# The last 24 units of a fused attention and feed-forward kernel in three chunks of 8, two of them with tokens on partitions

## The chip, the cores and the metric

The kernel runs on one core of a Trainium2 chip. The metric is device time in microseconds, the median of several runs. Beside it there is one profiled execution, with the times of every instruction and DMA piece; its own time is given with it.

## The reference

A polynomial-sketch attention feeds a feed-forward layer with a learned Swish. Cut to what matters here:

```python
batch, n_heads, seq, head_dim = (4, 4, 1088, 32)
attn_out = _attn_ref(q, k, v, S1, S2)                  # (4, 4, 1088, 32)
x = attn_out.transpose(0, 2, 1, 3).reshape(4352, 128)  # a token's four heads side by side

h = x @ w_in                                           # (4352, 128) @ (128, 2048)
g = h * (1.0 / (1.0 + np.exp(-beta * h)))              # beta: one for each of the 2048 columns
out = g @ w_out                                        # (4352, 2048) @ (2048, 128), f32
```

The attention phase makes `xall`, the 4352 tokens in f16 with the 128 model dimensions on partitions. The change lies in the second phase, the last three lines.

## The kernel before, in words

A sequence of 1088 tokens is cut into 34 units (`U`) of 32 tokens (`T`): token t of unit u is row `t * 34 + u` of the sequence. The four batches give 136 units. So 32 tokens of one unit lie 34 rows apart in the output, and rows of neighbouring units with the same t lie side by side.

The feed-forward phase works on chunks of units. `chunks` holds eight of 16 units (512 tokens) and a last one of 8 (256 tokens). A chunk has 16 blocks `j` of 128 hidden columns, handled in waves. A wave fills two PSUM banks, 1024 columns: two blocks of 512 tokens or four of 256. There are 68 waves in all: 64 of the first kind, 4 of the second.

- `first(s, w)`, steps `f<s>a` and `f<s>b`: half a wave each. TensorE multiplies `winb` (the input weights times beta) with `xall` into the PSUM tile `wave` (L705). After the b half ScalarE applies Silu to the 1024 columns and writes them as f16 into `gT` (L716). The very last wave is done in two Silus of 512 (L714). `wave` has two buffers.
- `second(s, w)`, steps `s<s>a` and `s<s>b`: half a wave of the product with `woutp`, summed over the 16 blocks in PSUM. For chunks of 16 units `woutp` is the stationary operand and the 512 tokens stream (L737); the result, in the tile `acc`, has model dimensions on partitions and tokens along the row. For the last chunk `gT` is stationary and the 128 columns of `woutp` stream (L729); the result, in the tile `fin` on two banks, has tokens on partitions, 128 in each bank.
- `store(ci)`, steps `o0` to `o8`. For a chunk of 16 units VectorE transposes `acc` in blocks of 32 by 32 into `osb` (L664). Then SP issues four DMAs, one for each 32 model dimensions (L670); a piece of them is 32 floats, 128 bytes. A chunk that crosses a batch boundary, such as chunk 6, takes two such groups, eight DMAs.
- `store_last`, step `o8`: ScalarE copies the first bank of `fin` and VectorE the second (L685), and each half goes out in one DMA (L686), the first on ScalarE's queue, the second on SP's. A piece is a whole row of 128 floats, 512 bytes. Partitions run over unit and then token, so the outer dimension of the output's access pattern is the 4 units and the next one the 32 tokens.

Nothing is left to a scheduler. `ORDER` is a list of step names written by hand, and each engine's program is the steps in that order. An engine stops at an instruction until the semaphores for its operands have come; instructions behind it on the same engine wait too. In the last part of `ORDER`, `f` steps run several waves ahead of the `s` steps, `o7` stands between `f67a` and `f67b`, and `s64a` to `s67b` and `o8` are last.

PSUM is full: `wave` takes two buffers of two banks, `att2` two banks, `acc` and `att1` one each. `fin` uses `att2`, which the attention phase has left by then.

Of the kernel before, what the change touches and what calls it, by code (L numbers as in the profile page):

```python
# [7 lines left out]
F32 = mybir.dt.float32  # L8
F16 = mybir.dt.float16
ALU = mybir.AluOpType  # L10
ACTF = mybir.ActivationFunctionType

P = 128
T = 32
# [3 lines left out]
def kernel(  # L18
# [12 lines left out]
    nc = tc.nc  # L31

    B, H, S, D = q.shape
    R = S1.shape[0]
    F = R * R
    NTOK, DM = out.shape
    DFF = moe_w_in.shape[1]
    NJ = DFF // P
    U = S // T
# [32 lines left out]
    f47a f47b s40b s41a s41b f48a f48b s42a s42b f49a f49b s43a s43b f50a f50b s44a s44b s45a f51a f51b s45b  # L72
    s46a f52a f52b s46b s47a s47b f53a f53b f54a o5 f54b s48a s48b s49a f55a f55b s49b s50a f56a f56b s50b s51a
    f57a f57b s51b s52a s52b f58a f58b s53a s53b f59a f59b s54a s54b s55a s55b f60a f60b f61a o6 f61b s56a s56b
    s57a s57b f62a f62b s58a s58b f63a f63b s59a s59b s60a f64a f64b s60b s61a f65a f65b s61b s62a s62b f66a
    f66b s63a s63b f67a o7 f67b s64a s64b s65a s65b s66a s66b s67a s67b o8
    """

    ENGINES = {
# [12 lines left out]
    ps = ctx.enter_context(tc.tile_pool(name="ps", bufs=1, space=bass.MemoryType.PSUM))  # L92
    ctx.enter_context(tc.manual_schedule())

    def ap(t, offset, dims, p0=0, pn=None):
        pd = list(t.ap[0])
        s = t if pn is None else t[p0 : p0 + pn]
        return bass.AP(tensor=s.tensor, offset=s.offset + offset, ap=[list(s.ap[0])] + dims)

    def ct(shape, dtype, name):  # L100
        return const.tile(shape, dtype, tag=name, name=name)
# [36 lines left out]
    att2_t = lambda n: ps.tile([P, 2, 512], F32, tag="att2", name=n)  # L138
    acc_t = lambda n: ps.tile([P, 512], F32, tag="acc", name=n)
# [501 lines left out]

    chunks = []
    u = 0
    for n in (16,) * 8 + (8,):
        chunks.append((u, n))
        u += n
    assert u == B * U and chunks[-1][1] == 8
    waves = []
    for ci, (u0, un) in enumerate(chunks):
        per = 1024 // (un * T)  # L650
# [2 lines left out]

    gts, accs, wvs = {}, {}, {}

    LAST = len(chunks) - 1

    def store(ci):
        u0, un = chunks[ci]
        if ci == LAST:  # L660
            store_last(u0, un)
            return
        osb = sb.tile([P, 16, T], F32, tag="osb", bufs=3, name="osb")
        nc.vector.transpose(out=osb[:, :un, :].rearrange("p u m -> p (u m)"), in_=accs[ci][:, : un * T])  # L664
        done = 0
        while done < un:
            b, u = divmod(u0 + done, U)
            n = min(un - done, U - u)
            for m in range(4):
                nc.sync.dma_start(  # L670
                    out=bass.AP(
                        tensor=out.tensor,
                        offset=out.offset + (b * S + u) * DM + m * T,
                        ap=[[U * DM, T], [DM, n], [1, T]],
                    ),
                    in_=osb[T * m : T * m + T, done : done + n, :],
                )
            done += n

    def store_last(u0, un):  # L680

        b, u = divmod(u0, U)
        for i, (copy, e) in enumerate(((nc.scalar.copy, nc.scalar), (nc.vector.tensor_copy, nc.sync))):
            o = ct([P, DM], F32, f"fin_sb{i}")
            copy(out=o, in_=accs[LAST][:, i, 0:DM])  # L685
            e.dma_start(  # L686
                out=bass.AP(
                    tensor=out.tensor,
                    offset=out.offset + (b * S + u + 4 * i) * DM,
                    ap=[[DM, 4], [U * DM, T], [1, DM]],  # L690
                ),
                in_=o,
            )

    def first(s, w):
        ci, n, per, j0 = waves[s]
        u0, un = chunks[ci]
        if s % GP == 0 and w == 0:
            gts[s // GP] = sb.tile([P, GP * 1024], F16, tag="gT", bufs=GB, name="gT")
        if w == 0:  # L700
            wvs[s] = wave_t("wave")
        half, g, o = per // 2, gts[s // GP], s % GP * 1024
        for i in range(half):
            j = j0 + w * half + i
            nc.tensor.matmul(  # L705
                out=wvs[s][:, w, i * n : i * n + n],
                lhsT=winb[:, j * P : j * P + P],
                rhs=xall[:, u0 * T : u0 * T + n],
                start=True,
                stop=True,  # L710
            )
        if s == len(waves) - 1 and w:
            for i in range(2):
                nc.scalar.activation(out=g[:, o + 512 * i : o + 512 * i + 512], in_=wvs[s][:, i], func=ACTF.Silu)  # L714
        elif w:
            nc.scalar.activation(  # L716
                out=g[:, o : o + 1024], in_=wvs[s].rearrange("p a n -> p (a n)"), func=ACTF.Silu
            )

    def second(s, w):  # L720
        ci, n, per, j0 = waves[s]
        if j0 == 0 and w == 0:
            accs[ci] = att2_t("fin") if ci == LAST else acc_t("acc")
        half = per // 2
        for i in range(half):
            j, o = j0 + w * half + i, s % GP * 1024 + w * 512 + i * n
            if ci == LAST:
                for a in range(2):
                    nc.tensor.matmul(  # L729
                        out=accs[ci][:, a, 0:DM],  # L730
                        lhsT=gts[s // GP][:, o + a * P : o + a * P + P],
                        rhs=woutp[:, j, :],
                        start=(j == 0),
                        stop=(j == NJ - 1),
                    )
                continue
            nc.tensor.matmul(  # L737
                out=accs[ci][:, :n],
                lhsT=woutp[:, j, :],
                rhs=gts[s // GP][:, o : o + n],  # L740
                start=(j == 0),
                stop=(j == NJ - 1),
            )

    for s in range(len(waves)):
        for w in range(2):
            step(f"f{s}{'ab'[w]}", first, s, w)
            step(f"s{s}{'ab'[w]}", second, s, w)
    for ci in range(len(chunks)):
        step(f"o{ci}", store, ci)  # L750
# [37 lines left out]
```

## Time and profile before

| | us |
|---|---|
| median of three runs | 104.2 (103.89, 104.2, 107.08) |
| profiled execution | 104.39 |
| its span, first to last instruction | 102.63 |
| TensorE busy in the span | 95.2 (93%) |
| ScalarE busy | 72.3 (70%) |
| VectorE busy | 59.1 (58%) |
| GpSimd busy | 40.7 (40%) |

The granted TensorE clock was 0.998 of full speed. The shares are means over two very different phases: GpSimd works in the attention phase alone, and in the last 20 us TensorE and ScalarE work with hardly a pause. The time outside the span, 1.75 us, is before the first and behind the last recorded instruction. A row of the groups reads: line, engine, operation, output and inputs, shapes, count, then busy time in us and mean ns of one, then the engine's idle time before these instructions and what ended it. A row of the DMA issues gives the KB of each and the median us from issue to landing. A matmul's duration in the rows is longer than its share of TensorE's time, since successive ones overlap; the distance between their starts is what counts.

### The profile page before, as it was taken

What the parts mean: (1) busy time and instruction counts of PE and PEld (TensorE: products, weight loads), DVE (VectorE), ACT (ScalarE), POOL (GpSimd) and SP (SyncE); (2) the same over time, 40 slices, a digit from 0 to 9 for tenths busy, and PEclk for the clock granted to TensorE, in tenths of its full rate; (3) what the DMA queues carried; (4) which work ended last, traced back from release to release, by engine and by line L of the source; (5) the groups of instructions that cost most, each with busy time, mean ns of one, the idle gap of its engine ahead of it and who ended that gap; (6) DMA issues with size and microseconds to landing.
All of it is one profiled execution on the core that took longest, in us unless ns stands there. A gap on an engine that the chain in (4) does not pass through costs nothing.

```text
span 102.6 us, 3065 instructions
## 1 busy us (share of the span) xinstructions
PE 95.2 (93%) x1294; PEld 45.0 (44%) x1294; DVE 59.1 (58%) x107; ACT 72.3 (70%) x92; POOL 40.7 (40%) x49
## 2 busy tenths in 40 slices
PE   5999989999999999999999999999999999999900
PEld 1234554344445454345446433644534444446800
DVE  1564888999798995898953967489240020200210
ACT  1412022687695984789995879999979999899710
POOL 6409689989997993008090000094000000000000
PEclk9999999999999999999999999999999999999999
DMA  2999999986661446613320261051004132022250
GB/s 50 321 255 306 394 378 386 246 270 134 248 217 32 90 127 174 169 27 64 94 70 13 43 114 60 0 101 39 6 13 70 19 52 50 0 44 49 44 101 25
DMA packets 24965, 12.56 MB, mean 122 GB/s; under 512 B 17992, under 2 KB 22648, under 8 KB 24952
## 3 DMA queue, kind: packets, MB, share of 16 engines
q1 hardware_dynamic: 24756, 12.29, 44.6%
q8 instruction: 10, 0.16, 0.7%
q10 hardware_dynamic: 196, 0.08, 0.3%
q14 instruction: 3, 0.02, 0.1%
HBM read 9.84 MB, written 2.23 MB: 118 GB/s over the span
## 4 chain that ended last, share of the span: by engine, by line
PE 86%; ACT 7%; DVE 1%; issue 1%; ACTq 0%
PE wave L705 27%; PE acc L737 24%; PE idle L340 9%; ACT gT L716 6%; PE at L520 6%; PE xp L571 5%; PE qpp L430 3%; PE kpp L357 2%; PE at L450 2%; PE fin L729 2%; PE at L393 2%; PE xw L571 1%; PE at L548 1%; PE at L407 1%; PE cb L393 0%
## 5 line engine op out<-in xcount | busy, mean ns | idle before, releaser
L716 ACT ACTIVATE gT<-wave 128x1024 f16<-128x1024 f32 x67 | 64.8, 1024 | 8.1 <-PE wave L705 7.5
L705 PE MATMUL wave<-xall,winb 128*128 128x512 f16 (+1 forms) x144 | 40.7, 368 | 0.4 <-DVE xall L588 0.2
L737 PE MATMUL acc<-gT,woutp 128*128 128x512 f16 x128 | 36.9, 379 | 0.0
L372 POOL TENSOR_TENSOR qp<-an,tq 128x768 f32<-128x768 f32 (+1 forms) x8 | 14.0, 1760 | 22.1 <-DVE an L496 22.1
L705 PEld LDWEIGHTS <-winb 128*128 128x128 f16 x144 | 13.4, 99 | 17.5 <-issue 3.9
L737 PEld LDWEIGHTS <-woutp 128*128 128x128 f16 x128 | 12.4, 98 | 14.9 <-issue 0.6
L664 DVE STREAM_TRANSPOSE osb<-acc 128x512 f32<-128x512 f32 x8 | 5.7, 714 | 21.1 <-PE acc L737 21.1
L372 POOL TENSOR_TENSOR kp<-tk 128x512 f32<-128x512 f32 (+1 forms) x12 | 15.0, 1276 | 6.4 <-DVE tk L368 6.4
L508 DVE STREAM_TRANSPOSE qpt<-qp 128x768 f32<-128x768 f32 (+1 forms) x13 | 11.1, 883 | 0.3 <-POOL qp L372 0.2
L340 PE MATMUL idle<-warm 128*128 128x512 f16 x30 | 9.6, 454 | 1.3 <-DVE tiny L231 1.3
L344 DVE STREAM_TRANSPOSE kT<-k_in 128x576 f32<-128x576 f32 (+1 forms) x8 | 5.6, 719 | 2.5 <-DMA k_in<-in_k_dram 2.5
L571 PE MATMUL xp<-qpt,kvr 32*32 32x288 f32 (+2 forms) x160 | 6.9, 364 | 0.0
L571 PE MATMUL xw<-qpt,kvr 32*32 32x256 f32 (+1 forms) x160 | 6.8, 343 | 0.0
L349 DVE STREAM_TRANSPOSE qT<-q_in 128x512 f32<-128x512 f32 (+1 forms) x8 | 5.8, 724 | 0.9 <-DMA q_in<-in_q_dram 0.9
L520 PE MATMUL at<-kp,v_in 128*32 128x64 f32 (+1 forms) x288 | 6.3, 223 | 0.0
L520 PEld LDWEIGHTS at<-kp,v_in 128*32 128x32 f32 (+1 forms) x288 | 4.7, 109 | 3.2 <-issue 1.7
L310 POOL TENSOR_TENSOR winb<-w_in_sb,beta_all 128x512 f16<-128x512 f32 x4 | 5.2, 1293 | 0.2 <-DMA beta_all<-in_moe_beta_dram 0.2
L340 PEld LDWEIGHTS <-warm 128*128 128x128 f16 x30 | 2.9, 110 | 4.5 <-issue 1.6
L571 PEld LDWEIGHTS xp<-qpt,kvr 32*32 32x32 f32 x160 | 3.7, 103 | 2.3 <-issue 0.8
L372 DVE TENSOR_TENSOR qp<-an,tq 128x768 f32<-128x768 f32 (+1 forms) x5 | 4.5, 906 | 0.1
L588 ACT CAST xall<-xw 128x128 f16<-128x128 f32 (+1 forms) x8 | 2.4, 325 | 3.0 <-PE xw L571 2.0
L473 DVE TENSOR_TENSOR prod<-tq,tcc 128x288 f32<-128x288 f32 (+2 forms) x5 | 4.1, 818 | 0.1
(75 smaller groups left out, 67.3 us busy)
## 6 DMA issues: line engine op xcount, KB each, us to landing
k_in<-in_k_dram SPq DMA_DIRECT2D x6, 272.0 KB, 5.3
q_in<-in_q_dram SPq DMA_DIRECT2D x6, 272.0 KB, 3.9
out_dram<-osb SPq DMA_DIRECT2D x20, 64.0 KB, 1.9
v_in<-in_v_dram SPq DMA_DIRECT2D x8, 144.0 KB, 4.0
v_in<-in_v_dram SPq DMA_DIRECT2D x8, 128.0 KB, 3.0
w_in_sb<-in_moe_w_in_dram SPq DMA_DIRECT2D x4, 256.0 KB, 4.8
beta_all<-in_moe_beta_dram SPq DMA_DIRECT2D x4, 256.0 KB, 6.9
w_out_sb<-in_moe_w_out_dram SPq DMA_DIRECT2D x4, 256.0 KB, 6.1
```

The source lines that it names most:

```text
L310: eng(name).tensor_tensor(out=winb[:, s], in0=w_in_sb[:, s], in1=beta_all[:, s], op=ALU.mult)
L340: nc.tensor.matmul(out=t[:, 0, :], lhsT=warm[:, 0:P], rhs=warm, start=True, stop=True)
L344: nc.vector.transpose(out=kT[:, u0:u1, :].rearrange("p u t -> p (u t)"), in_=k_in[b][:, u0 * D : u1 * D])
L349: nc.vector.transpose(out=qT[:, u0:u1, :].rearrange("p u t -> p (u t)"), in_=q_in[b][:, u0 * D : u1 * D])
L372: eng.tensor_tensor(out=ap(o, g0 * F, [[F, n], [R, R], [1, R]]), in0=ap(a, g0 * a_step + a_off, [[a_step, n], [1, R], [0, R]]), in1=ap(bsr ...
L508: nc.vector.transpose(out=ap(st[b]["qpt"], c0 * H * F, [[1, (c1 - c0) * H * F]]), in_=ap(st[b]["qp"], c0 * H * F, [[1, (c1 - c0) * H * F]]),)
L520: nc.tensor.matmul(out=t[T * h : T * h + T, :], lhsT=v_in[b][:n, h, c, :], rhs=kp[:n, 4 * c + h, :], start=(done == 0), stop=(done == NC - 1),
L571: nc.tensor.matmul(out=ts[j][T * h : T * h + T, 0 : n * T], lhsT=st[b]["kvr"][p : p + T, f, h, :], rhs=ap(st[b]["qpt"], (4 * c0 + h) * F + ...
L664: nc.vector.transpose(out=osb[:, :un, :].rearrange("p u m -> p (u m)"), in_=accs[ci][:, : un * T])
L705: nc.tensor.matmul(out=wvs[s][:, w, i * n : i * n + n], lhsT=winb[:, j * P : j * P + P], rhs=xall[:, u0 * T : u0 * T + n], start=True, sto ...
L716: nc.scalar.activation(out=g[:, o : o + 1024], in_=wvs[s].rearrange("p a n -> p (a n)"), func=ACTF.Silu)
L737: nc.tensor.matmul(out=accs[ci][:, :n], lhsT=woutp[:, j, :], rhs=gts[s // GP][:, o : o + n], start=(j == 0), stop=(j == NJ - 1),)
```

## The change

Chunks are now seven of 16 units and three of 8. Waves stay 68: 56 of two blocks, 12 of four. The old chunk 7 (16 units) becomes chunk 7 and chunk 8 of 8 units each; the last one is chunk 9.

The last two chunks are `turned`: their second product has `gT` as the stationary operand, so tokens lie on partitions. Silu writes their `gT` in another order: within 128 columns (four units) element (unit i, token t) goes to column `4 * t + i`. So a partition of the result is token * 4 + unit, and the output's access pattern begins with the 32 tokens, then the 4 units, then the row. Each of these two chunks goes out in two DMAs of 128 rows. Chunk 8's sums are in `att2`, its copies both on VectorE, its DMAs both on SP. Chunk 9's sums are in two tiles of one bank each, in the places of `acc` and `att1`; ScalarE copies and issues the first, VectorE and SP the second. Chunk 7 is stored as the chunks of 16 units are, with half the columns.

In `ORDER`, `o7` comes right behind `s59b`, `o8` behind `s63b`, and `o9` is last. The order of all `f` and `s` steps is the same. TensorE's program has 48 more matmuls, each with its weight load.

```diff
-    s57a s57b f62a f62b s58a s58b f63a f63b s59a s59b s60a f64a f64b s60b s61a f65a f65b s61b s62a s62b f66a
-    f66b s63a s63b f67a o7 f67b s64a s64b s65a s65b s66a s66b s67a s67b o8
+    s57a s57b f62a f62b s58a s58b f63a f63b s59a s59b o7 s60a f64a f64b s60b s61a f65a f65b s61b s62a s62b f66a
+    f66b s63a s63b o8 f67a f67b s64a s64b s65a s65b s66a s66b s67a s67b o9
...
-    for n in (16,) * 8 + (8,):
+    for n in (16,) * 7 + (8, 8, 8):
...
+    turned = (LAST - 1, LAST)
+
+    def turned_acc(ci):
+        if ci < LAST:
+            t = att2_t("fin")
+            return t[:, 0], t[:, 1]
+        return acc_t("fin0"), ps.tile([P, 512], F32, tag="att1", name="fin1")
...
-    def store_last(u0, un):
-
-        b, u = divmod(u0, U)
-        for i, (copy, e) in enumerate(((nc.scalar.copy, nc.scalar), (nc.vector.tensor_copy, nc.sync))):
-            o = ct([P, DM], F32, f"fin_sb{i}")
-            copy(out=o, in_=accs[LAST][:, i, 0:DM])
-            e.dma_start(
+    def store_turned(ci):
+        b, u = divmod(chunks[ci][0], U)
+        for i in range(2):
+            own_queue = ci == LAST and i == 0
+            o = ct([P, DM], F32, f"fin_sb{ci}{i}")
+            (nc.scalar.copy if own_queue else nc.vector.tensor_copy)(out=o, in_=accs[ci][i][:, 0:DM])
+            (nc.scalar if own_queue else nc.sync).dma_start(
                 out=bass.AP(
                     tensor=out.tensor,
                     offset=out.offset + (b * S + u + 4 * i) * DM,
-                    ap=[[DM, 4], [U * DM, T], [1, DM]],
+                    ap=[[U * DM, T], [DM, 4], [1, DM]],
                 ),
                 in_=o,
             )
...
-        if s == len(waves) - 1 and w:
-            for i in range(2):
-                nc.scalar.activation(out=g[:, o + 512 * i : o + 512 * i + 512], in_=wvs[s][:, i], func=ACTF.Silu)
-        elif w:
-            nc.scalar.activation(
-                out=g[:, o : o + 1024], in_=wvs[s].rearrange("p a n -> p (a n)"), func=ACTF.Silu
-            )
+
+        m = 2 if s == len(waves) - 1 else 1
+        for i in range(m if w else 0):
+            d, k = g[:, o + i * 512 : o + i * 512 + 1024 // m], 8 // m
+            x = wvs[s].rearrange("p a n -> p (a n)")[:, i * 512 : i * 512 + 1024 // m]
+            if ci in turned:
+                d = ap(g, o + i * 512, [[P, k], [1, 4], [4, T]])
+                x = x.rearrange("p (a i t) -> p a i t", i=4, t=T)
+            nc.scalar.activation(out=d, in_=x, func=ACTF.Silu)
...
-            accs[ci] = att2_t("fin") if ci == LAST else acc_t("acc")
+            accs[ci] = turned_acc(ci) if ci in turned else acc_t("acc")
...
-            if ci == LAST:
+            if ci in turned:
                 for a in range(2):
                     nc.tensor.matmul(
-                        out=accs[ci][:, a, 0:DM],
+                        out=accs[ci][a][:, 0:DM],
                         lhsT=gts[s // GP][:, o + a * P : o + a * P + P],
```

More of the change, by code (lines that the diff above doesn't have):

```diff
@@ L643 @@
     u = 0
-    for n in (16,) * 8 + (8,):
+    for n in (16,) * 7 + (8, 8, 8):
         chunks.append((u, n))
         u += n
-    assert u == B * U and chunks[-1][1] == 8
+    assert u == B * U
     waves = []
@@ L656 @@
     LAST = len(chunks) - 1
+    turned = (LAST - 1, LAST)
[4 more added lines that the diff above has]
+        return acc_t("fin0"), ps.tile([P, 512], F32, tag="att1", name="fin1")
     def store(ci):
         u0, un = chunks[ci]
-        if ci == LAST:
-            store_last(u0, un)
+        if ci in turned:
+            store_turned(ci)
             return
@@ L726, in second @@
             j, o = j0 + w * half + i, s % GP * 1024 + w * 512 + i * n
-            if ci == LAST:
+            if ci in turned:
                 for a in range(2):
                     nc.tensor.matmul(
-                        out=accs[ci][:, a, 0:DM],
+                        out=accs[ci][a][:, 0:DM],
                         lhsT=gts[s // GP][:, o + a * P : o + a * P + P],
```

## The prediction

> **What bounds the kernel now.** I read the page's chain first, then the timeline of the last microseconds, then the busy shares in half-microsecond windows, then the DMA issues. The chain says which engine sets the end of the computation:
>
> ```profile
> PE 86%; ACT 7%; DVE 1%; issue 1%; ACTq 0%
> ...
> 95.27 0.44 PE wave L705 x4
> 95.71 1.80 PE fin L729 x32
> 97.51 0.02 issue
> 97.53 0.28 ACT fin_sb L685
> 97.81 0.02 issue
> 97.83 0.29 DVE fin_sb L685
> ```
>
> TensorE is on the path to 97.51 us, back to back since 82.43; then two copies, one after the other. The chain ends at 98.12, the span at 102.6. The missing 4.5 us are the last stores, which the chain does not follow, so I look there. The timeline from 97 on:
>
> ```profile
> 97.53 0.27 ACT L685 COPY fin_sb<-fin 128x128 f32<-128x128 f32 x1 [0.65 <-PE fin L729]
> 97.83 0.65 ACTq L686 DMA_DIRECT2D out_dram<-fin_sb  x1
> 97.83 0.29 DVE L685 COPY fin_sb<-fin 128x128 f32<-128x128 f32 x1 [1.80 <-ACT fin_sb L685]
> 98.15 0.70 SPq L686 DMA_DIRECT2D out_dram<-fin_sb  x1
> ```
>
> VectorE's copy is released by ScalarE's copy, not by TensorE: the halves share one tile and are served in turn. The store issued last starts at 98.15. The windows (times, length, five engines, clock, DMA share, GB/s) show how it drains:
>
> ```profile
> 98.50:99.00 0.50, 0.00 (x0) 0.00 (x0) 0.00 (x0) 0.00 (x0) 0.00 (x0) 1.00 0.77 131
> 99.00:99.50 0.50, 0.00 (x0) 0.00 (x0) 0.00 (x0) 0.00 (x0) 0.00 (x0) 1.00 0.17 43
> 99.50:100.00 0.50, 0.00 (x0) 0.00 (x0) 0.00 (x0) 0.00 (x0) 0.00 (x0) 1.00 0.28 81
> 100.00:100.50 0.50, 0.00 (x0) 0.00 (x0) 0.00 (x0) 0.00 (x0) 0.00 (x0) 1.00 0.28 78
> 100.50:101.00 0.50, 0.00 (x0) 0.00 (x0) 0.00 (x0) 0.00 (x0) 0.00 (x0) 1.00 0.20 60
> ```
>
> To 99.0 the 16 DMA engines are 77% busy: that is o7, 2048 pieces of 128 B, issued on SP from 96.05 to 97.99. Then the two last stores move 128 KB at a share of 0.2 to 0.28, four engines of sixteen. Their outer dimension is 4 (the units), and each has four landing events, the last at 100.56 (ScalarE's) and 101.32 (SP's); the stores of `osb`, whose outer dimension is 32 (the tokens), have sixteen. From 101.32 to 102.63 runs the end of the program.
>
> **The change, part by part**, against the profiled execution: 104.39 us, of which 102.63 in the span.
>
> *TensorE, +0.1 us on the path.* The number of waves stays 68. Eight waves are formed from four matmuls of 256 columns in place of two of 512: by the chain a wave of four takes 0.44, of two 0.43, so 0.01 x 8. Chunk 7's second product has 16 matmuls of 256 for eight of 512: same pitch (about 0.11 and 0.22). Chunk 8's becomes 32 matmuls of 128: 1.80 us as for `fin` above, against 8 x 0.216 = 1.73. Bounds 0 to 0.2 (the longer weight loads of these rows lie beside the matmuls in the trace); I take 0.1.
>
> *Silu writes every fourth element, taken as 0.* The last eight waves (seven instructions of 1024 and two of 512) write two-byte values 8 bytes apart. No row of before does that. The lower end is the rows as they are:
>
> ```profile
> L716 ACT ACTIVATE gT<-wave 128x1024 f16<-128x1024 f32 x67 | 64.8, 1024 | 8.1 <-PE wave L705 7.5
> L714 ACT ACTIVATE gT<-wave 128x512 f16<-128x512 f32 x2 | 1.1, 598 | 0.0
> L588 ACT CAST xall<-xw 128x256 f16<-128x256 f32 x4 | 1.4, 374 | 2.7 <-PE xw L571 1.7 <-PE xp L571 1.0
> L559 ACT COPY kvr<-at 128x256 f32<-128x256 f32 x1 | 0.4, 373 | 0.8 <-PE at L548 0.8
> L473 DVE TENSOR_TENSOR prod<-tq,tcc 128x288 f32<-128x288 f32 x3 | 2.4, 815 | 0.1
> L496 DVE TENSOR_TENSOR an<-tq,rden 128x288 f32<-128x288 f32 x3 | 1.3, 445 | 0.1
> ```
>
> The cast of L588 writes two-byte runs of 32 with gaps and costs 374 ns, the straight copy of as many elements 373: broken writes cost ScalarE nothing there. The upper end is VectorE's product that leaves a gap after every eight elements, 815 against 445, a factor of 1.83, or +0.85 us for each full Silu. ScalarE's own row is the nearer; I take 0 and keep 0.85 for a rival. On the size of the step I look in the Trainium skill, "SBUF — State Buffer", in the note on cachelines: lines have 16 bytes and full rate needs two accesses per line. Eight-byte steps make exactly two, so by that page too the sum has 0 here, but a step twice as wide would not; no run yet shows it.
>
> *Copies side by side, -0.3 us.* The last two halves lie in two tiles (the banks of `acc` and `att1`), and VectorE's copy waits for TensorE alone. Both start at TensorE's end: 97.83 becomes 97.53, and SP can issue at 97.85 + 0.1 = 97.95 instead of 98.15. If the two readers still took turns, this gain would be 0.
>
> *The last stores over sixteen engines, -1.55 us.* The outer dimension becomes 32. From issue to landing SP's store took 101.32 - 98.15 = 3.17. The nearest rows with an outer dimension of 32:
>
> ```profile
> out_dram<-osb SPq DMA_DIRECT2D x20, 64.0 KB, 1.9
> out_dram<-osb SPq DMA_DIRECT2D x4, 16.0 KB, 1.5
> ```
>
> The new store has 128 pieces like the 16 KB row, of 512 B like `fin` now; such pieces follow each other on an engine every 0.0235 us. Eight per engine take 0.19, in place of 32 x 0.0235 = 0.75 behind ScalarE's 32 on the same four. The 512-piece row's 1.9 is one bound, 1.5 the other; from 1.5, plus 0.1 for the larger pieces, I take 1.62. The landing is then 97.95 + 1.62 = 99.57. Here the skill has a price that speaks against so large a gain: "DMA: Bandwidth & Descriptors", in its anatomy of one DMA, gives about 2.0 us fixed plus bytes / 436 GB/s, for the GpSimd path; estimated so, 64 KB takes 2.15, the landing is at 100.1 and the time 103.2. The two rows above, both below 2.0, are why I do not take it.
>
> *o7 and o8 leave the tail, 0 on the path.* VectorE: a transpose of 256 elements for o7 (441 ns by the L442 row of that shape) behind s59b, and two copies of 0.29 for o8 behind s63b; it is otherwise idle there. SP: o7's four issues were waiting for 95.31 + 0.72; now they are ready at 92.7, but SP issues o6 until 94.43. Then four of about 0.45 with gaps of 0.05 end at 96.3; o8's two, 0.45 to 0.70 each, end at 97.3 to 97.8. The last issue needs SP at 97.95: covered by 0.15 to 0.65. If that cover is gone, each tenth that SP is late is a tenth of the end.
>
> *Sum.* Last landing 101.32 -> 99.57, and 1.31 behind it as now: the span becomes 100.9, the time 104.39 - 1.75 = 102.64. The median of the runs shown is 104.2, 0.2 under the profiled run, so 102.45 against that. I say 102.6; the bounds above (0 to 0.2, 0 to 0.3, 1.5 to 1.9) give 102.1 to 103.2.
>
> **Rivals.** *(1) The stepped write slows ScalarE; slower.* ScalarE is 6.92 of 7.2 us busy in 85 to 92.2 and 3.29 of 3.3 after it, so it has no room: the last Silu ends at 96.88, the first weight load that needs it starts at 97.06. Eight waves x 0.85 - 0.17 = 6.6 us, 109.2. It decides early: (1.75 + 0.17) / 8 = 0.24 per Silu uses up the gain (1.26 us), 0.49 makes it 2% slower. Against it: the equal casts.
>
> *(2) SP is late.* One issue at 91.28 took 1.64 us instead of 0.45, while a 16 KB instruction transfer (queue q8, from 91.17 to 92.52) ran; the trace has ten of these, the last ones 12 and 17 us apart, and SP's long issues of 1.2 to 1.6 us all end about 0.39 behind one. TensorE's program grows by 96 instructions, so the next can come before the end: in 96 to 98 it costs 0.3 to 1.2 us, 103.3. For it: the cover is only 0.15 to 0.65. Against it: before had none in its last 10 us.
>
> *(3) A store's fixed part is most of it.* The landing takes 1.9 to 2.2 as for 64 KB now: 102.9 to 103.2. For it: 512 small pieces and 128 differ by 0.4 only.
>
> *(4) The fan-out stays at four*, because the partitions now run token, unit: then only the copies and the queue behind o7 are gained (the first 512 B piece moves at 99.12, just after o7's last at 99.00). About 0.4 us: 104.0.
>
> **How the numbers follow.** 2% of 104.2 is 2.1 us, about what a measurement of this kernel tells from no change. Forecast 0.60, at 102.6; rival 1 0.10, most of it beyond 2%; rival 2 0.16; rival 3 0.08; rival 4 0.06. Faster by over 2% needs a time under 102.1, the low end of the forecast's own range, where run-to-run differences of 0.2 add: 0.16. Slower by over 2% is rival 1 less its mild part: 0.09. The rest, 0.75, lies within. The range 101.9 to 104.0 holds the forecast's bounds and rivals 2 to 4, and leaves out rival 1 and a gain over 2.3.
>
> **What would show it.** Right: sixteen landing events for each of the last stores; VectorE's last copy released by PE and starting with ScalarE's; the last issue near 97.9 and nothing moving after 99.5; Silu of 1024 at 1.02 us in both forms; TensorE's end within 0.2 of 97.5. Wrong: a stepped Silu over 1.2 us with TensorE waiting on it; an SP issue over 1 us behind 95; four landing events; landings 2 us and more behind their issue.

## The result: 113.6 us, 8.6% slower

The changed kernel takes 113.61 us (median of five runs, 113.03 to 115.8) against 104.88 for the kernel before beside it: ratio 1.086, interval 1.078 to 1.094. Now and then an execution of any kernel here comes a few per cent late (one of the five of each kernel here, two of the four of e1); such runs are left out of the ratios, and of the times given below.

The profiled execution is 113.41 us, its span 111.70, 9.07 more than before. The groups by shape (line, engine, operation, shapes, count, busy us, mean ns):

```profile
L728 ACT ACTIVATE gT<-wave 128x1024 f16<-128x1024 f32 x67 | 74.2, 1180 | 7.9 <-PE wave L713 7.4
L728 ACT ACTIVATE gT<-wave 128x512 f16<-128x512 f32 x2 | 2.5, 1392 | 0.0
L739 PE MATMUL fin<-woutp,gT 128*128 128x128 f16 x64 | 5.2, 225 | 2.0 <-ACT gT L728 2.0
L713 PE MATMUL wave<-xall,winb 128*128 128x256 f16 x48 | 7.8, 292 | 5.6 <-ACT gT L728 5.6
```

The 1180 mixes two kinds of Silu of one shape: sixty at 1.02 us, and the seven that write in steps, at 2.44 to 2.54 in the trace. The two of 512 columns went from 598 to 1392 ns. TensorE now waits for `gT` (L739) and for `wave` to come free (L713), which it did not before. The chain over the last 23 us says the same:

```profile
88.43 0.45 PE wave L713 x4
88.88 0.02 issue
88.90 0.02 ACTq L728
88.92 0.04 issue
88.97 8.02 ACT gT L728 x4
96.98 1.00 issue
97.98 9.37 ACT gT L728 x5
107.34 0.05 issue
107.39 0.41 PE fin L739 x4
107.80 0.02 issue
107.82 0.29 DVE fin_sb L693
```

Up to 88.9 the two kernels run alike. From the first stepped Silu on ScalarE is the path; the entry of 1.00 "issue" lies inside the stretch in which ScalarE was busy without a break. The last Silu ends at 107.34, where it ended at 96.88 before: +10.46 us. Behind it the change does gain: from the last Silu's end to the end of the span 4.37 us in place of 5.76. The sum is +9.07.

The tail itself, by the timeline and by windows (times, length, five engines, clock, DMA share, GB/s):

```profile
107.77 0.27 ACT L693 COPY fin_sb<-fin 128x128 f32<-128x128 f32 x1 [0.43 <-PE fin L739]
107.82 0.29 DVE L693 COPY fin_sb<-fin 128x128 f32<-128x128 f32 x1 [5.70 <-PE fin L739]
108.06 0.64 ACTq L694 DMA_DIRECT2D out_dram<-fin_sb  x1
108.14 0.54 SPq L694 DMA_DIRECT2D out_dram<-fin_sb  x1
```

```profile
109.00:109.50 0.50, 0.00 (x0) 0.00 (x0) 0.00 (x0) 0.00 (x0) 0.00 (x0) 1.00 0.25 74
109.50:110.00 0.50, 0.00 (x0) 0.00 (x0) 0.00 (x0) 0.00 (x0) 0.00 (x0) 1.00 0.66 189
```

Both copies are released by TensorE, 0.05 us apart. The stores run at up to 0.66 of the sixteen engines and 189 GB/s, where they had 0.28 and 81, and each has sixteen landing events.

### The profile page after: what moved, and what is told of

It reads as the page before. It is cut to its first block, busy times and chain, and to the rows that moved or that the text cites. A ratio compares the mean times of both kernels' runs of the same rounds, so it can differ in the third digit from the quotient of the medians.

```text
span 111.7 us, 3167 instructions
## 1 busy us (share of the span) xinstructions
PE 97.7 (88%) x1342; PEld 49.4 (44%) x1342; DVE 59.0 (53%) x109; ACT 83.0 (74%) x92; POOL 40.7 (36%) x49
## 4 chain that ended last, share of the span: by engine, by line
PE 68%; ACT 22%; DMA 3%; issue 2%; DVE 2%; ACTq 0%
PE wave L713 22%; ACT gT L728 22%; PE acc L747 19%; PE at L520 5%; PE xp L571 5%; PE idle L340 4%; DMA k_in<-in_k_dram 3%; PE qpp L430 2%; PE at L450 2%; PE kpp L357 2%; PE at L393 1%; PE xw L571 1%; DVE kT L344 1%; PE at L548 1%; PE at L407 1%
## 5 line engine op out<-in xcount | busy, mean ns | idle before, releaser
L728 ACT ACTIVATE gT<-wave 128x1024 f16<-128x1024 f32 (+1 forms) x69 | 76.5, 1186 | 7.9 <-PE wave L713 7.4
L713 PE MATMUL wave<-xall,winb 128*128 128x512 f16 (+1 forms) x160 | 41.5, 353 | 6.0 <-ACT gT L728 5.6
L747 PE MATMUL acc<-gT,woutp 128*128 128x512 f16 (+1 forms) x128 | 35.2, 370 | 0.0
L713 PEld LDWEIGHTS <-winb 128*128 128x128 f16 x160 | 15.2, 101 | 22.7 <-issue 10.6
L672 DVE STREAM_TRANSPOSE osb<-acc 128x512 f32<-128x512 f32 (+1 forms) x8 | 5.4, 680 | 21.7 <-PE acc L747 21.7
L340 PE MATMUL idle<-warm 128*128 128x512 f16 x30 | 9.1, 439 | 1.3 <-DVE tiny L231 1.3
L739 PE MATMUL fin<-woutp,gT 128*128 128x128 f16 x64 | 5.2, 225 | 2.0 <-ACT gT L728 2.0
L693 DVE COPY fin_sb<-fin 128x128 f32<-128x128 f32 x3 | 0.8, 288 | 11.3 <-PE fin L739 11.3
L739 PEld LDWEIGHTS <-gT 128*128 128x128 f16 x64 | 4.2, 102 | 2.8 <-ACT gT L728 2.6
L588 ACT CAST xall<-xw 128x128 f16<-128x128 f32 (+1 forms) x8 | 2.4, 325 | 3.4 <-PE xw L571 2.0
```

Source lines behind the costliest of these rows:

```text
L340: nc.tensor.matmul(out=t[:, 0, :], lhsT=warm[:, 0:P], rhs=warm, start=True, stop=True)
L713: nc.tensor.matmul(out=wvs[s][:, w, i * n : i * n + n], lhsT=winb[:, j * P : j * P + P], rhs=xall[:, u0 * T : u0 * T + n], start=True, sto ...
L728: nc.scalar.activation(out=d, in_=x, func=ACTF.Silu)
L739: nc.tensor.matmul(out=accs[ci][a][:, 0:DM], lhsT=gts[s // GP][:, o + a * P : o + a * P + P], rhs=woutp[:, j, :], start=(j == 0), stop=(j ...
L747: nc.tensor.matmul(out=accs[ci][:, :n], lhsT=woutp[:, j, :], rhs=gts[s // GP][:, o : o + n], start=(j == 0), stop=(j == NJ - 1),)
```

## The experiments

The theory: the whole loss is the price of Silu's stepped f16 write; the rest of the change gains what was forecast. Rivals: the three small chunks or the early stores cost too; any access out of order is dear; the stretch as a whole, or its clock, is slow.

**The write in order again (e1).** The Silu lines with the step are gone, and the two stores of each of chunks 8 and 9 have the units outermost again:

```diff
-            if ci in turned:
-                d = ap(g, o + i * 512, [[P, k], [1, 4], [4, T]])
-                x = x.rearrange("p (a i t) -> p a i t", i=4, t=T)
...
-                    ap=[[U * DM, T], [DM, 4], [1, DM]],
+                    ap=[[DM, 4], [U * DM, T], [1, DM]],
```

> The chunks, the order of steps, the tiles and the copies are those of the change; only Silu writes its columns in order again, and the stores of chunks 8 and 9 have the 4 units as outer dimension again. Theory (the write order of Silu is the whole loss): Silu of 1024 at 1.02 us everywhere, TensorE's end near 97.6, and a time of 103.9 to 104.4, ratio 0.995 to 1.00: the copies run side by side (-0.3) but each last store still drains through four engines. Rival (three small chunks, the earlier stores or the extra matmuls cost as well): 106 or more, up to the 113 of the changed kernel if the write order is harmless.

Measured: 104.12 and 104.22, against 104.1 before; span 102.40. Silu is back at its old time:

```profile
L725 ACT ACTIVATE gT<-wave 128x1024 f16<-128x1024 f32 x67 | 64.8, 1024 | 7.9 <-PE wave L713 7.3
```

So the small chunks, their early stores and 48 more matmuls cost nothing that shows. The run takes out two things, the write order and the new outer dimension of the stores; e5, which keeps the stores, shows that the write order is the loss.

**The order made by TensorE's read (e2).**

```diff
-                rhs=xall[:, u0 * T : u0 * T + n],
+                rhs=ap(xall, u0 * T, [[P, 2], [1, T], [T, 4]]) if ci in turned else xall[:, u0 * T : u0 * T + n],
```

> The order token * 4 + unit is made by TensorE, which reads the 256 columns of its moving operand in steps of 32 f16 elements (64 bytes); Silu writes in order, the stores are those of the change. Theory (only ScalarE's write order is slow): matmuls of 256 columns keep their distance of 0.11 us, Silu takes 1.02, and with the 3.9 us that the changed kernel needs from TensorE's end to the span's end the time is 102.7 to 103.3, ratio 0.985 to 0.99. Rival (a stepped read is as dear on TensorE): 32 matmuls at twice the distance add 3.5 us, 106.5; the rival that the stores of the change themselves cost: over 104.5 with Silu and matmuls at their old times.

Measured: 114.39, ratio 1.099 (1.092 to 1.106). Silu was back at 1024 ns, but the step had only moved. The chain of this kernel:

```profile
87.85 3.44 PE wave L713 x8
91.29 0.88 PE acc L744 x8
92.17 1.72 PE wave L713 x4
```

Four stepped matmuls of 256 columns take 1.72 us, 0.43 each, where the plain ones take 0.44 for all four: four times, not the twice of my rival. 32 x 0.32 = 10.2 us.

**The order made by Silu's read of PSUM (e5).** The same permutation, with the step on the other side of the same instruction:

```diff
-                d = ap(g, o + i * 512, [[P, k], [1, 4], [4, T]])
-                x = x.rearrange("p (a i t) -> p a i t", i=4, t=T)
+                d = d.rearrange("p (a t i) -> p a t i", i=4, t=T)
+                x = x.rearrange("p (a i t) -> p a t i", i=4, t=T)
```

> The order token * 4 + unit is made by Silu's read: it reads PSUM in steps of 32 f32 elements (128 bytes) and writes in order. All else is the change. Theory (the write side is the dear one): Silu 1.02 to 1.1 us, time 102.7 to 103.5, ratio 0.985 to 0.995. Rival (any out-of-order access of ScalarE is dear): Silu near 2.5 us and a time near 113, ratio 1.08.

Measured: 102.98, ratio 0.989 (0.984 to 0.995). It does everything the change meant to do, and is 1.1% under the kernel before: clear of the noise, but a small gain. ScalarE reads f32 from PSUM in steps of 128 bytes at no price: 1024 ns.

```profile
L728 ACT ACTIVATE gT<-wave 128x1024 f16<-128x1024 f32 x67 | 64.8, 1024 | 7.9 <-PE wave L713 7.3
97.52 0.27 ACT L693 COPY fin_sb<-fin 128x128 f32<-128x128 f32 x1 [0.61 <-PE fin L739]
97.57 0.29 DVE L693 COPY fin_sb<-fin 128x128 f32<-128x128 f32 x1 [1.73 <-PE fin L739]
```

**What a stepped write costs (e4).** Behind the end of the kernel before, the pattern is repeated by itself; `stepped(4)` is the change's:

```diff
+    def stepped(n):
+        return [[1, n], [n, 512 // n]], [[512 // n, n], [1, 512 // n]]
+    def runs(r):
+        return [[r, 2], [2 * r, 256 // r], [1, r]], [[256, 2], [r, 256 // r], [1, r]]
...
+    pats = [flat, stepped(2), stepped(4), stepped(8), stepped(16), runs(2), runs(4), runs(8), read]
+    for eng, t in ((a_silu, w16), (a_silu, w32), (a_copy, w16), (v_copy, w16), (v_copy, w32)):
+        for dims, xdims in pats:
+            dummy(eng, t, 0, dims, xdims)
```

> The kernel before, with 45 operations on 512 elements each added behind its end, nine patterns each for Silu to f16 and f32 and copy to f16 on ScalarE and copy to f16 and f32 on VectorE: in order, steps of 2, 4, 8 and 16 elements, runs of 2, 4 and 8 elements in steps of twice the run, and a write in order of elements read in steps of 128. The output is that of the kernel before; the time is not to be compared. Theory A (two accesses in one line of 16 bytes are enough): f16 steps of 2 and 4 and f32 steps of 2 at the 0.60 us of the plain Silu, wider ones slower. Theory B (any write whose predecessor is not its neighbour is slow): every step from 2 on costs the 1.39 us of the changed kernel, runs of 2 lie halfway, runs of 8 near 0.7. Theory C (two-byte writes alone): f16 as in B, f32 steps all at 0.60. The read in steps: 0.60 by A, B and C, 1.39 if order itself is dear on either side.

The timeline, first Silu to f16 in order, then in steps of 2, 4, 8 and 16 elements and in runs of 2; then to f32 in steps of 2 and 4; then VectorE's cast to f16 in steps of 2, 4 and 8:

```profile
98.82 0.60 ACT L767 ACTIVATE warm<-wave 128x512 f16<-128x512 f32 x1 [0.72 <-ACT fin_sb L685]
99.44 0.74 ACT L767 ACTIVATE warm<-wave 128x512 f16<-128x512 f32 x1
100.22 1.30 ACT L767 ACTIVATE warm<-wave 128x512 f16<-128x512 f32 x1
101.55 2.43 ACT L767 ACTIVATE warm<-wave 128x512 f16<-128x512 f32 x1
104.01 2.30 ACT L767 ACTIVATE warm<-wave 128x512 f16<-128x512 f32 x1
106.34 0.60 ACT L767 ACTIVATE warm<-wave 128x512 f16<-128x512 f32 x1
...
109.35 0.62 ACT L767 ACTIVATE q_in<-wave 128x512 f32<-128x512 f32 x1
110.00 1.07 ACT L767 ACTIVATE q_in<-wave 128x512 f32<-128x512 f32 x1
...
126.33 0.72 DVE L773 CAST warm<-wave 128x512 f16<-128x512 f32 x1
127.08 1.29 DVE L773 CAST warm<-wave 128x512 f16<-128x512 f32 x1
128.41 2.42 DVE L773 CAST warm<-wave 128x512 f16<-128x512 f32 x1
```

None of A, B and C holds. Take off the 0.172 us that the plain Silus have beside their 0.832 ns for each element (1.024 and 0.598 for 1024 and 512). Single f16 elements 4, 8 and 16 bytes apart touch 128, 256 and 512 pieces of 16 bytes, and the rest is 4.41 ns for each piece in all three (0.565, 1.129 and 2.259 us). The step of 16 elements touches 512 pieces too and takes no more, 2.30: the pieces touched count, not the distance. f32 elements 8 and 16 bytes apart touch 256 and 512, and the rest is 1.75 ns for each (0.447 and 0.895). Pairs of f16 in steps of 8 bytes fill whole words of 4 bytes, and cost 0.597 as in order: a step of 8 bytes is free for them. VectorE pays the same, so the price lies with the write to SBUF and not with ScalarE. The change's 1024 columns touch 512 pieces: 0.17 + 512 x 4.41 ns = 2.43 us; the first was 2.44, the others, which start 0.25 us before the one ahead of them ends, 2.53. The Trainium skill's note on cachelines ("SBUF — State Buffer"), by which two accesses in 16 bytes are enough, fits the f32 rows (0.62 against 0.59) and not the f16 write (1.30 against 0.60).

**Whole words in place (e7).** The change's order, written as pairs:

```diff
+                for h in range(2):
+                    nc.scalar.activation(
+                        out=ap(g, o + i * 512 + 2 * h, [[P, k], [4, T], [1, 2]]),
+                        in_=ap(wvs[s], i * 512 + 2 * T * h, [[P, k], [1, T], [T, 2]]),
+                        func=ACTF.Silu,
+                    )
```

> The change, but Silu writes the same out-of-order columns in whole words of 4 bytes: each Silu is cut in two, and each half writes neighbouring pairs of f16 elements in steps of 8 bytes (read from PSUM in steps). Theory (isolated two-byte writes are the dear thing, not the step of 8 bytes nor the order): a half of 512 takes 0.60, a wave 1.0 in place of 0.92 us, eight waves add 0.6 to 0.8 less the slack of 0.17: 103.4 to 103.8. Rival (any write with a step of 8 bytes is dear): halves of 1.39, 2.6 us for a wave, 115 or more.

Measured: 103.37, ratio 0.993 (0.990 to 0.996). The fourteen halves of 512, in steps of 8 bytes:

```profile
L727 ACT ACTIVATE gT<-wave 128x512 f16<-128x512 f32 x14 | 7.0, 625 | 0.3 <-PE wave L713 0.3
```

So in the kernel too, neither the order nor the step is dear, but the two bytes alone in their word.

**Half the dose (e8).** Chunk 8 as in e5, chunk 9 with the change's write.

> The change with the stepped write of Silu in chunk 9 alone (chunk 8 gets the same order by the read). Theory (each stepped wave costs its own time on a saturated ScalarE): the last Silu of eight stepped waves came 10.46 us later than before, so four add about 5.2: 108.0 to 108.5. Rival (the start of the stepped stretch, or the lower TensorE clock in it, sets the loss): near 113, or below 106.

Measured: 108.38, ratio 1.040 (1.035 to 1.046). The chain shows the four Silus of chunk 8, which write in order, and then the five stepped ones of chunk 9's four waves:

```profile
88.89 3.78 ACT gT L731 x4
92.67 0.03 issue
92.70 9.28 ACT gT L731 x5
```

The last Silu ends at 101.97, 5.09 behind the kernel before: half of 10.46. The price is paid wave by wave.

**The last chunk alone (e6).** The kernel before with the order by the read, the outer dimension of 32 and two tiles for the last chunk; the chunks, `ORDER` and o7 unchanged:

```diff
-            accs[ci] = att2_t("fin") if ci == LAST else acc_t("acc")
+            accs[ci] = fin_t() if ci == LAST else acc_t("acc")
...
-                    ap=[[DM, 4], [U * DM, T], [1, DM]],
+                    ap=[[U * DM, T], [DM, 4], [1, DM]],
```

> The kernel before with one part of the change alone: chunks, their order and o7 as before; the last chunk of 8 units has its order token * 4 + unit (made by Silu's read of PSUM), its stores have the 32 tokens as outer dimension, and its two halves lie in two tiles. Theory (the fan-out of the last stores and the copies side by side are nearly the whole gain of the repaired kernel): 103.0 to 103.4; SP is busy with o7 until 98.0 and the last pieces queue behind o7's until 99.0, so up to 0.3 us behind the repaired kernel's 102.98. Rival (splitting the 16 units and storing them early is what counts): 103.8 to 104.2, near the kernel before.

Measured: 102.97, ratio 0.987 (0.982 to 0.993), the same as e5. Splitting the 16 units and storing them early gains nothing that shows: here SP's last issue is at 97.97 instead of 97.89, and the last landing at 99.97 instead of 100.06.

**What stepped reads cost (e9).** Behind the end of the kernel before, reads of SBUF in steps.

> The kernel before with reads of SBUF in steps added behind its end, 512 elements each: as TensorE's moving operand in f16 (in order, steps of 2, 4, 8 and 32, runs of 2 and of 4), by Silu from f16 and f32, by VectorE's copy from f16 (in order, steps of 2, 4, 8, 32). The output is that of the kernel before; the time is not to be compared. Theory (reads have a price for each line of 16 bytes that is touched, 1.68 ns by the 0.43 us of a stepped matmul of 256 columns): TensorE 0.22 in order and with steps of 2, 0.43 at 4, 0.86 at 8 and 32, runs of 4 in steps of 8 still 0.43; Silu 0.60 up to f16 steps of 4 and f32 steps of 2, near 1.04 beyond. Rival (any step is dear on TensorE alone): 0.86 for all steps there, 0.60 for Silu throughout.

At full clock successive matmuls of 512 columns start 0.216 us apart in order, 0.226 with f16 steps of 2, 0.452 at 4 and 0.900 at 8: from a step of 2 on, 1.76 ns for each 16 bytes touched. Runs of 4 in steps of 8 take 0.226; the 0.43 that I wrote for them was a slip, since four elements share a line there. Runs of 2 in steps of 4 fell into a stretch of half the granted clock, 0.427 apart; their one distance at full clock is 0.225. Silu from SBUF is free up to f16 steps of 4 and f32 steps of 2 (0.657 and 0.654 us against 0.63) and takes 1.10 at twice that. So TensorE and ScalarE read at one price, that of whole-word writes; isolated two-byte writes cost 2.5 times as much. VectorE's copy of f16 does not follow that price: it takes 0.295 in order, 0.43 at steps of 2 and 4 and 0.672 at 8, where 512 x 1.75 ns alone would be 0.90.

## Why the prediction was wrong, and where it was right

*The step that failed is "Silu writes every fourth element, taken as 0".* I chose the nearer of two rows, the cast of L588, because it was ScalarE's own and wrote f16 with gaps. But its runs are 32 elements, 64 bytes, whole words and whole lines; it could say nothing about single f16 elements. The upper end was too low as well: VectorE's 1.83 was a row of f32 runs, and need not come from their gaps (in e4 VectorE's f32 runs of 8 with gaps took 0.691, in order 0.679); the real factor was 2.5, +1.51 us for a full Silu where I had 0.85. So the range could not hold the time even where it listed the cause.

*Rival 1 was the outcome*, and its mechanism was right: ScalarE had no room, and the loss came wave by wave (e8). It put the point where it decides at 0.24 us for each Silu, and the measured 1.51 was six times that. Its price, 6.6, was 10.46 by the runs. That is less than eight times 1.51, since successive Silus overlap: from start to start they took 2.26 us in place of 0.94, the eight waves 10.70 longer in all, and they began 0.24 earlier than before. It had a chance of 0.10: a cost that no row bounded, on an engine with no slack, should have had more. Reading the Trainium skill's note on cachelines ("SBUF — State Buffer") as a second witness did not help: by its two accesses for each line eight bytes were just allowed, and e4 shows twice the time there (1.30 against 0.60).

*The other terms*, by e5, where the write is repaired. TensorE +0.1: the copies start at 97.52 in place of 97.53, nothing was lost. Copies side by side: the issue came as forecast, at 97.89 for 97.95, but no run shows by itself that this reached the end, for the store that lands last is now ScalarE's, issued at 97.81 where it was 97.83 before. Stores over sixteen engines: the fan-out is right and is nearly the whole gain (e1 against e5: 104.2 and 103.0), but 1.62 us from issue to landing was too short:

```profile
out_dram<-fin_sb SPq DMA_DIRECT2D x3, 64.0 KB, 2.0
out_dram<-fin_sb ACTq DMA_DIRECT2D x1, 64.0 KB, 2.2
```

SP's last store took 1.90, with an issue of 0.54; ScalarE's, issued 0.08 earlier, took 2.24 and is now the last to land, because its pieces run from 99.36 to 99.70, behind SP's from 99.08 to 99.44 on the same engines. The last landing is 100.06 against the 99.57 forecast, and the 102.98 measured against 102.6 is this term: rival 3 described it, with 102.9 to 103.2. For the last landing the 2.15 estimated from the Trainium skill's fixed cost ("DMA: Bandwidth & Descriptors", the anatomy of one DMA) was nearer than my 1.62; SP's 1.90 is that of the 512-piece row. The bounds of the terms, added up again, give 102.2 to 103.1 against the median, not the 102.1 to 103.2 that I wrote; that changes nothing here.

*o7 and o8, 0 on the path*: right; SP's last issue for o8 ended at 97.30, 0.59 before it was needed. *Rival 2* did not come: SP's one long issue, 1.12 us, was at 89.77. *Rival 4* is out by the sixteen landings.

## What to carry to other kernels

Before an engine writes out of order, look at what lies together in 4 and in 16 bytes: two-byte elements that are alone in their word cost 4.41 ns for every 16 bytes touched, on ScalarE and VectorE alike, while the same permutation costs ScalarE nothing as a stepped read of f32 from PSUM (e5). An edit on an engine that is busy to the last per cent needs a price from its own pattern; where no row shows that pattern, the chance has to go to the unknown, not to the row that looks most alike. And where a last store is slow, look at its outer dimension first: 4 to 32 took 1.2 us off the end here (e1 against e5).

## What was not expected of the hardware

The prices for each 16 bytes in e4 and e9 (4.41 ns for lone two-byte writes, 1.75 for words, 1.76 for TensorE's moving read) were new to me, and so was a pair of f16 being free where a single one costs twice. The granted TensorE clock fell to half for stretches of 3.4 us or more in the kernels that ran long at the end (in the changed one from 93.3 to 96.7). In e2, from 100.3 to 107.1, it took the plain matmuls of `fin` from 0.056 to 0.107 us each and left the stepped ones at 0.430: at either clock their price is the same. What sets off the lower clock was not tried.
